# A linear-attention and expert-attention kernel: the last batch's output rows in another buffer, and the last store's second half on another queue

## The chip, the core and the metric

The kernel runs on one core of a Trainium2 chip. The metric is the device time of one execution, in microseconds (us), lower is better. The engines are named as in the profile: PE is TensorE's matmul part and PEld its weight loads, DVE is VectorE, ACT is ScalarE, POOL is GpSimd and SP is SyncE, which here does nothing but issue transfers (DMAs) and wait. An engine's name with a q behind it (SPq, ACTq) means its sequencer, the part that takes instructions in program order, waits for semaphores and issues DMAs.

## What is computed

Two blocks follow each other, for 8 batches of 576 tokens. The first is linear attention without a softmax, normed per head. The second gives its output, as a 576 x 512 matrix, to four attention experts of which each token uses two. Cut to what matters:

```python
kv = np.einsum('bhsd,bhse->bhde', k, v)
out = np.einsum('bhsd,bhde->bhse', q, kv)
x = out / np.sqrt(np.mean(out * out, -1, keepdims=True) + 1e-06) * g_norm
# x as (8, 576, 512); logits = x @ w_gate; the two largest of four, softmax w
for e in range(4):
    a = softmax(causal(scale * (x @ wq[e]) @ (x @ wk[e]).T))
    result += w[e] * (a @ (x @ wv[e]) @ wo[e])     # only where e was chosen
```

The result is 8 x 576 x 512 float32, 9.44 MB, and it is written to HBM block by block.

## The kernel before, in words

A batch's 576 tokens are cut into five blocks: four of 128 and one of 64 (`blocks`, L141). Each step of the work is a small function that emits a few instructions for one batch and one block or head pair. The order in which steps are emitted is written out by hand in the string `ORDER` (L27), the engine that does a copy in `ENGINE` (L53), and the number of the buffer that each new tile gets in `SLOTS` (L67). Each engine runs its own instructions in the order of emission. A step that takes a buffer waits until what had been in it is read.

The buffers of interest:

- `buf(key, ...)` (L174): the first use of a key takes the next digit of `SLOTS`, and the tile lies in the SBUF buffer named after the key's first word and that digit. A tile for `("y", b, qc)` is one output block, 128 x 512 float32, and there are four such buffers, y0 to y3. Those for `("k", b)` hold a whole batch of k, 8 KB in each of 128 partitions, and there are two, k0 and k1.
- PSUM has eight banks, which `small` (L169) hands out by the same string. `own_waits` (L812) makes a step wait for other engines' earlier use of its bank.

The end of each batch is what the change touches. For each head pair, `pv` (L699) multiplies the attention weights with v, `rc`, `iv` and `oc2` (L721, L725, L731) scale the result into the tile `osc`, `ot` (L745) transposes it on TensorE, and `ot_copy` (L753) moves the transposed piece into `OT`. For the last batch, `ot` and `ot_copy` are split in two parts, of the blocks 0 to 2 and 3 to 4. Then, for each of the five blocks, `y_mm` (L758) multiplies by the output weights into a PSUM bank, `y_copy` (L769) copies the bank into a y buffer (on ACT or DVE, as `ENGINE` says), and `store` (L773) issues the transfer to HBM on SP. The block of 64 tokens is computed as two halves of 256 columns, which lie one above the other on 128 partitions, so its store is two transfers of 64 KB each.

The steps at the end of the last two batches (6 and 7) are emitted in the order below; the engine of a copy stands in brackets, and the y buffer that it takes behind it. "y 7,1" is `y_mm` of batch 7 and block 1, "yc" its copy and "st" its store.

```
yc 6,4 [DVE] y2   yc 6,3 [DVE] y1   yc 6,2 [ACT] y3   yc 6,1 [ACT] y0
y 6,0  ...  yc 6,0 [ACT] y2    st 6,0
y 7,1    y 7,2    yc 7,1 [ACT] y1
ot 7,1,1    y 7,0    otc 7,1,1 [ACT]    st 7,1    yc 7,2 [DVE] y3
y 7,4    st 7,2    yc 7,0 [ACT] y0    y 7,3    st 7,0
yc 7,3 [ACT] y2    st 7,3    yc 7,4 [DVE] y1    st 7,4 (two transfers)
```

So the copy of block 7,4 takes the buffer y1 that block 7,1 had. Some PSUM banks matter too: y 6,0 and y 7,2 use the same bank, so y 7,2 starts when yc 6,0 has read it.

The k buffers at that time: k1 held batch 6's k, which the matmuls of `kv` (L397, profile line L405) read; the last matmuls of that line start at 152.4 us.

Of the kernel before, what the change touches and what calls it, by code (L numbers as in the profile page):

```python
# [10 lines left out]
FP32 = mybir.dt.float32  # L11
# [5 lines left out]
NB, NCH, EP, NF = 5, 4, 2, 4  # L17
# [51 lines left out]
    "03213023001450125330041553671046715124206076504703012002312304131301521310305463730144000161154030511021123100"  # L69
    "21032031300212304020355310033454230511002671100030021301312130131233012011162710120630302105741002011007622113"  # L70
    "76237645370022034133033513001020167021101712013140501230131220522000011345101132110062711036712067201230130130"
    "0130210201126701672451030121067001267145340621"
)


# [43 lines left out]
def kernel(  # L119
# [13 lines left out]
    nc = tc.nc  # L133
    P = nc.NUM_PARTITIONS
    B, H, S, Dh = q.shape
    D = H * Dh
# [14 lines left out]
    tiles = {}  # L151
# [6 lines left out]
    def place(key):  # L158
        if key not in slot_of:
            slot_of[key] = int(SLOTS[begun[0]])  # L160
            begun[0] += 1
        return slot_of[key]
# [6 lines left out]
    def small(*key):  # L169
        n = place(("sm",) + key)  # L170
        touched.add(n)
        return pairs[n // 2][:, n % 2, :]

    def buf(key, shape, dtype, name):  # L174
        if key not in tiles:
            n = place(key)
            tiles[key] = sb.tile(shape, dtype, tag=f"{key[0]}{n}", name=f"{name}{n}")
        return tiles[key]
# [102 lines left out]
    def copy(task, dst, src):  # L281
        if engine[task] == "A":
            nc.scalar.copy(dst, src)  # L283
        else:
            nc.vector.tensor_copy(out=dst, in_=src)  # L285
# [472 lines left out]
    def y_mm(b, qc):  # L758
        p_y, (s0, nq) = small("y", b, qc), blocks[qc]
        for pr in range(EP):  # L760
            lhs = OTs[b % 2][:, pr * S + s0 : pr * S + s0 + nq]
            for o in range(P // nq):
# [3 lines left out]
                    start=(pr == 0), stop=(pr == EP - 1), skip_group_check=True,  # L766
                )

    def y_copy(b, qc):  # L769
        w = D * blocks[qc][1] // P  # L770
        copy(("yc", b, qc), buf(("y", b, qc), [P, D], FP32, "y")[:, 0:w], small("y", b, qc)[:, 0:w])

    def store(b, qc):  # L773
        s0, nq = blocks[qc]
        for o in range(P // nq):
            w = D * nq // P
            nc.sync.dma_start(out[b, s0 : s0 + nq, o * w : (o + 1) * w], tiles["y", b, qc][o * nq : (o + 1) * nq, 0:w])

    emit = dict(
        lk=lk, lv=lv, lkr=lkr, lvr=lvr, lq=lq, gr=gr, g8=g8, gb=gb, wg=wg, lw=lw, ws=ws, lwo=lwo, wo=wo,  # L780
# [1 line left out]
        out=out_mm, oc=o_copy, sq=square, red=red, ln=ln, rs=rs, na=newton_a, nb=newton_b, nc=newton_c, nd=newton_d, gl=gl, lg=lg, xm=xm, x=x_tr, xc=x_copy,  # L782
        m8=m8, sh=sh, ex=ex, md=md, mk=mk, gt=gt, den=den, rd=rd, gate=gate, v=v_mm, vc=v_copy,
        qp=lambda b, pr: proj("q", b, pr), kp=lambda b, pr: proj("k", b, pr), qpc=q_proj_copy, kpc=k_proj_copy,
        sc=sc, exp=exp, msk=msk, pv=pv, rc=rc, iv=ivm, oc2=o_scale, ot=ot, otc=ot_copy, y=y_mm, yc=y_copy, st=store,
    )

# [78 lines left out]
```

## Time and profile before

| what | value |
|---|---|
| median of four runs | 226.44 us (225.45 to 227.54) |
| the profiled execution's own time | 225.64 us |
| its span, first to last instruction | 223.9 us |
| PE busy | 208.6 us (93% of the span) |
| DVE busy | 157.6 us (70%) |
| ACT busy | 133.2 us (59%) |
| POOL busy | 126.0 us (56%) |
| stores of results | 48 transfers, all issued by SP |
| HBM written | 9.44 MB |

The profiled execution is 0.80 us below the median. What lies outside its span (225.64 - 223.9) is 1.74 us. The timeline gives each instruction, or run of like instructions, with its start and duration in us from the span's start; "[2.00 <-DMA ...]" behind it is the time for which its engine sat idle before it, and what ended that. A DMA row of SPq or ACTq is the issue alone; the time from the start of the issue to the landing of the data is a view of its own.

### The profile page before, as it was taken

To read this page: it belongs to the slowest core of one execution; us is meant where nothing else is said; L and a number is where in the kernel's file an instruction comes from. 1 tells how busy PE (TensorE), PEld (TensorE's weight loads), DVE (VectorE), ACT (ScalarE), POOL (GpSimd) and SP (SyncE) were. 2 spreads that over 40 slices of the span, in tenths; PEclk is the share of its full clock that TensorE was granted. 3 is DMA by queue.
4 is the path that set the end of the run, shared out by engine and by line. 5 is a ranking of instruction groups with operands and counts; after the bars stand their busy time and mean duration, and the time that the engine had idled before them with its cause. 6 is when DMAs were issued, how large, how long until landed. Compare 5 with 4: busy or idle time off the path is not lost. (4 is left out here: it accounts for less than half of the span.)

```text
span 223.9 us, 6608 instructions
## 1 busy us (share of the span) xinstructions
PE 208.6 (93%) x2550; PEld 177.5 (79%) x2562; DVE 157.6 (70%) x366; ACT 133.2 (59%) x265; POOL 126.0 (56%) x278
## 2 busy tenths in 40 slices
PE   7788799998999989999999999999999999999981
PEld 2467697987998889898997899788878999799550
DVE  6275669749665988789797675499996476843570
ACT  0214742876679462868426954956764982664951
POOL 8400776069538681669607960577649779621620
PEclk9999999999999999999999999999999999999998
DMA  4979979999999879999999899997234000140065
GB/s 124 316 231 259 296 190 221 353 241 128 142 336 241 152 177 273 187 187 218 220 249 241 268 224 234 146 225 157 62 104 147 3 0 4 46 165 3 0 220 207
DMA packets 92577, 40.29 MB, mean 180 GB/s; under 512 B 66689, under 2 KB 88193, under 8 KB 92545
## 3 DMA queue, kind: packets, MB, share of 16 engines
q1 hardware_dynamic: 90784, 38.68, 71.3%
q10 hardware_dynamic: 1632, 1.18, 2.0%
q8 instruction: 20, 0.33, 0.7%
q14 instruction: 13, 0.10, 0.2%
q0 software_dynamic: 128, 0.01, 0.0%
HBM read 30.42 MB, written 9.44 MB: 178 GB/s over the span
## 5 line engine op out<-in xcount | busy, mean ns | idle before, releaser
L686 ACT ACTIVATE PT<-p 128x1024 bf16<-128x1024 f32 (+1 forms) x64 | 50.3, 841 | 6.6 <-PE p L672 6.1
L692 POOL TENSOR_SCALAR_AFFINE_SELECT PT<-PT 128x256 bf16<-128x256 bf16 (+1 forms) x80 | 29.3, 384 | 26.2 <-ACT PT L686 24.9
L557 POOL TENSOR_TENSOR x_tok<-o_sb,rstd 128x512 fp32r<-128x512 f32 x40 | 43.1, 1131 | 0.5
L466 PE MATMUL p<-kvx,qT 128*128 128x136 f32 (+1 forms) x320 | 39.3, 285 | 1.1 <-DVE kvx L285 0.7
L466 PEld LDWEIGHTS p<-kvx,qT 128*128 128x128 f32 (+1 forms) x320 | 34.7, 179 | 3.9 <-DVE kvx L285 0.9
L502 DVE TENSOR_REDUCE ms<-sq 128x8 f32<-128x520 f32 (+1 forms) x40 | 27.0, 684 | 7.5 <-POOL sq L498 3.7
L498 POOL TENSOR_TENSOR sq<-o_sb 128x512 f32<-128x512 f32 (+1 forms) x20 | 20.6, 1041 | 12.6 <-DVE ms L502 6.4
L626 PE MATMUL p<-wv_r,xT 128*128 128x256 f32 x160 | 25.2, 292 | 0.7 <-ACT xT L283 0.7
L567 PE MATMUL p<-ident_r,x_tok 128*128 128x128 f32 (+1 forms) x160 | 23.4, 279 | 0.7 <-DVE vext L285 0.3
L567 PEld LDWEIGHTS p<-ident_r,x_tok 128*128 128x128 f32 x160 | 20.6, 191 | 3.7 <-POOL x_tok L557 1.0
L672 PE MATMUL p<-qTp,kT 64*128 64x64 f32 (+4 forms) x192 | 21.8, 341 | 1.2 <-DVE kT L285 0.5
L283 ACT COPY o_sb<-p 128x544 f32<-128x544 f32 (+1 forms) x29 | 15.1, 532 | 13.0 <-PE p L466 12.5
L626 PEld LDWEIGHTS p<-wv_r,xT 128*128 128x128 f32 x160 | 20.9, 189 | 1.9 <-ACT xT L283 0.8
L645 PE MATMUL p<-xT,wk_r 128*128 128x288 f32 x128 | 20.8, 305 | 0.0
L405 PE MATMUL p<-v_b,k_b 128*64 128x64 f32 x512 | 20.1, 224 | 0.1
L764 PE MATMUL p<-wo_b,OT 128*128 128x512 bf16 (+1 forms) x85 | 18.3, 343 | 1.8 <-issue 0.5
L645 PE MATMUL p<-xT,wq_r 128*128 128x288 f32 x128 | 19.8, 300 | 0.0
L405 PEld LDWEIGHTS p<-v_b,k_b 128*64 128x64 f32 x512 | 17.8, 138 | 2.5 <-issue 2.1
L672 PEld LDWEIGHTS p<-qTp,kT 64*128 64x128 f32 x192 | 14.1, 185 | 6.3 <-ACT PT L686 1.5
L645 PEld LDWEIGHTS p<-xT,wk_r 128*128 128x128 f32 x128 | 17.6, 188 | 1.5 <-DVE xT L285 0.5
L285 DVE COPY o_sb<-p 128x544 f32<-128x544 f32 (+1 forms) x19 | 12.0, 630 | 9.5 <-PE p L466 4.2
L645 PEld LDWEIGHTS p<-xT,wq_r 128*128 128x128 f32 x128 | 17.5, 188 | 0.4 <-issue 0.4
(111 smaller groups left out, 345.5 us busy)
## 6 DMA issues: line engine op xcount, KB each, us to landing
out_dram<-y SPq DMA_DIRECT2D x32, 256.0 KB, 2.7
k_b<-in_k_dram SPq DMA_DIRECT2D x14, 512.0 KB, 5.9
v_b<-in_v_dram SPq DMA_DIRECT2D x14, 512.0 KB, 5.8
q_b<-in_q_dram SPq DMA_DIRECT2D x48, 144.0 KB, 4.7
q_b<-in_q_dram SPq DMA_DIRECT2D x16, 128.0 KB, 3.8
k_b<-in_k_dram SPq DMA_DIRECT2D x4, 256.0 KB, 5.5
v_b<-in_v_dram ACTq DMA_DIRECT2D x4, 256.0 KB, 5.4
k_rem<-in_k_dram SPq DMA_DIRECT2D x16, 64.0 KB, 4.5
```

Source lines behind the costliest of these rows:

```text
L405: nc.tensor.matmul(p_kv[hh * Dh : (hh + 1) * Dh, c, :], lhsT=lhs, rhs=rhs, start=(j == 0), stop=(j == NF), skip_group_check=True,)
L466: nc.tensor.matmul(p_o[p0 : p0 + nt, c // 2, c % 2 * 256 : c % 2 * 256 + 2 * GW], lhsT=qTs[b % NQT][:, c * S + i * P : c * S + i * P + nt] ...
L498: nc.gpsimd.tensor_tensor(out=dst, in0=src, in1=src, op=AluOpType.mult)
L502: nc.vector.tensor_reduce(mss[b % 2][:nt, i, :], sqs[(NB * b + i) % 3][:nt], axis=AX_X, op=AluOpType.add)
L557: nc.gpsimd.tensor_tensor(out=buf(("x", b, i), [P, NCH, P], FP32R, "x_tok")[:].rearrange("p c (h r) -> p h r c", h=H), in0=ob[:, i, :, 0:D ...
L567: nc.tensor.matmul(p_t[:, c * P : c * P + nt], lhsT=tiles["x", b, i][:, c, :], rhs=ident_r[:, 0:nt], start=True, stop=True)
L626: nc.tensor.matmul(p_v[:, 0 : E * Hd], lhsT=blocks_of(xTs[b % 2], c)[:, i * P : (i + 1) * P], rhs=w_r["v"][:, c, :, :].rearrange("p e f -> ...
L645: nc.tensor.matmul(p_p[:, s, 0:HALF], lhsT=w_r[nm][:, c, 2 * pr : 2 * pr + 2, :].rearrange("p e f -> p (e f)"), rhs=blocks_of(xTs[b % 2], ...
L672: nc.tensor.matmul(p_s[:, el, o : o + hi - lo], lhsT=kTs[(2 * b + pr) % 3][pp, kb * P : (kb + 1) * P], rhs=tiles["qTp", b, pr][pp, lo:hi], ...
L686: nc.scalar.activation(PT[:, :, d0 : d0 + o], big("sc", b, pr, j)[:, :, 0:o], ACTF.Exp, scale=scale)
L692: nc.gpsimd.affine_select(out=d, in_=d, compare_op=AluOpType.is_ge, fill=0.0, base=0, pattern=[[0, 2], [1, w]], channel_multiplier=-1,)
L764: nc.tensor.matmul(p_y[o * nq : (o + 1) * nq, 0:w], lhsT=lhs, rhs=wo_b[:, pr, o * w : (o + 1) * w], start=(pr == 0), stop=(pr == EP - 1), ...
```

## The change

Blocks 0 to 3 of the last batch no longer take four y buffers. They share one tile in buffer k1, [128, 4, 512] float32, a slice for each block, and block 4 of the last batch is then the only one of its batch in a y buffer. With three fewer buffer requests, the end of `SLOTS` is shorter: the last digits now give k1 to the shared tile, and still give y1 to block 7,4. The order of the steps and the engines of the copies are as they were. The second of the two transfers of the last block's store (`o` = 1, columns 256 to 511, partitions 64 to 127) is issued by ACT in place of SP; it stands behind yc 7,3 in ACT's order.

```diff
-    "0130210201126701672451030121067001267145340621"
+    "0130210201126701672451030121067001267145461"
 )
...
+    def y_t(b, qc):
+        if b == B - 1 and qc < NF:
+            return buf(("k", "y"), [P, NF, D], FP32, "k_b")[:, qc]
+        return buf(("y", b, qc), [P, D], FP32, "y")[:]
+
     def y_copy(b, qc):
         w = D * blocks[qc][1] // P
-        copy(("yc", b, qc), buf(("y", b, qc), [P, D], FP32, "y")[:, 0:w], small("y", b, qc)[:, 0:w])
+        copy(("yc", b, qc), y_t(b, qc)[:, 0:w], small("y", b, qc)[:, 0:w])
 
     def store(b, qc):
         s0, nq = blocks[qc]
         for o in range(P // nq):
             w = D * nq // P
-            nc.sync.dma_start(out[b, s0 : s0 + nq, o * w : (o + 1) * w], tiles["y", b, qc][o * nq : (o + 1) * nq, 0:w])
+            eng = nc.scalar if b == B - 1 and o else nc.sync
+            eng.dma_start(out[b, s0 : s0 + nq, o * w : (o + 1) * w], y_t(b, qc)[o * nq : (o + 1) * nq, 0:w])
```

## The prediction, made before the change was run

> **What bounds the kernel now.** The page comes first, to see whether the change can reach the bulk of the time:
>
> ```profile
> span 223.9 us, 6608 instructions
> PE 208.6 (93%) x2550; PEld 177.5 (79%) x2562; DVE 157.6 (70%) x366; ACT 133.2 (59%) x265; POOL 126.0 (56%) x278
> PE   7788799998999989999999999999999999999981
> DMA  4979979999999879999999899997234000140065
> ```
>
> PE is 93% busy and full in nearly every slice up to the last two. The change moves nothing that PE does and nothing ahead of the last batch's output, so those 216 us stay. What it can touch is the last slice and a half, where PE falls to 8 and 1: a drain of matmuls, copies and stores. Next, therefore, the chain that ended last, in order of time, from 216 us:
>
> ```profile
> 216.01 0.70 PE p L764 x2
> 216.78 0.59 ACT y L283
> 217.39 2.06 DMA out_dram<-y
> 219.63 0.42 DVE y L285
> ```
>
> This reads: block 7,1's matmuls, its copy on ACT, its store to HBM, and then the copy of block 7,4, which needs the y buffer that this store had to read. It looks as if that wait set the end. Whether it does is decided by SP, so I read the timeline of the same stretch, engine by engine (ACT, DVE, PE), and then SP's three last issues, each in a window of its own:
>
> ```profile
> 216.12 1.24 ACT L283 COPY y<-p 128x512 f32<-128x512 f32 x2 [2.00 <-DMA out_dram<-y]
> 218.00 0.32 ACT L283 COPY OT<-p 128x192 bf16<-128x192 bf16 x1 [0.64 <-PE p L764]
> 218.22 0.59 ACT L283 COPY y<-p 128x512 f32<-128x512 f32 x1
> 219.40 0.59 ACT L283 COPY y<-p 128x512 f32<-128x512 f32 x1 [0.59 <-PE p L764]
> ...
> 217.46 0.69 DVE L285 COPY y<-p 128x512 f32<-128x512 f32 x1 [0.88 <-PE p L764]
> 219.63 0.42 DVE L285 COPY y<-p 128x256 f32<-128x256 f32 x1 [1.49 <-DMA out_dram<-y]
> ```
>
> ```profile
> 218.37 0.41 PE L764 MATMUL p<-wo_b,OT 128*64 128x256 bf16 x4 [0.46 <-ACT OT L283]
> ...
> 218.71 0.60 PE L764 MATMUL p<-wo_b,OT 128*128 128x512 bf16 x2
> ```
>
> ```profile
> 220.01 0.33 SPq L777 DMA_DIRECT2D out_dram<-y  x1
> ...
> 220.43 0.47 SPq L777 DMA_DIRECT2D out_dram<-y  x1
> ...
> 220.96 0.59 SPq L777 DMA_DIRECT2D out_dram<-y  x1
> ```
>
> The reader is to see two things. First, two copies waited for a store's landing: yc 6,0 (216.12) and yc 7,4 (219.63). Second, SP takes its stores in order, and st 7,3 stands ahead of st 7,4. It cannot be issued before yc 7,3 ends on ACT (219.40 + 0.59 = 219.99); it goes at 220.01 and takes 0.33, and the two halves of st 7,4 follow at 220.43 and 220.96. yc 7,4 had ended at 219.63 + 0.42 = 220.05, so it lay finished for 0.38 us before SP got to it. The end is set by yc 7,3 and three issues in a row. The views of time to landing for these three windows give 2.0, 1.9 and 2.0 us: the last data land at 220.96 + 2.0 = 223.0, and 0.9 us of closing instructions bring the span to 223.9.
>
> **The buffer part, step by step.**
> - yc 7,1 (ACT, 216.78): it follows yc 6,0, which ends at 216.12 + 0.59 = 216.71, and its matmuls end at 216.01 + 0.70 = 216.71 too. A free buffer can give at most the 0.07 us in between; I take 0. Its new wait is for the last reader of k1: matmuls of line L405, which start no later than 152.4 us, 64 us earlier. Behind it on ACT stand the OT copy and yc 7,0, so a late one would be felt; it isn't late.
> - yc 7,2 (DVE, 217.46): its idle time is ended by PE. 0.
> - yc 7,0 (ACT, 218.22): it starts while the OT copy (218.00 + 0.32) still ends, back to back. 0.
> - yc 7,3 (ACT, 219.40): ended by PE, whose matmuls finish at 218.71 + 0.60 = 219.31. 0.
> - yc 7,4 (DVE): its matmuls end at 218.37 + 0.41 = 218.78. DVE's previous copy started about 0.08 us after PE was done (217.46 against 216.76 + 0.60 = 217.36), so it starts near 218.87 in place of 219.63 and ends near 219.29, 0.76 us earlier. Nothing waits for it but st 7,4, which SP can't issue before 220.43. So on the path this is 0: the in-order store of 7,3 is the cover, and what is late next.
> - yc 6,0 keeps its buffer y2, whose store (st 6,4) it waited for. That stall stays, and it matters: y 7,2 takes the PSUM bank that yc 6,0 reads. The waits after 215.9 us have it:
>
> ```profile
> ACT y L283 <- DMA out_dram<-y: 2.0, 1, 2.0
> DVE y L285 <- DMA out_dram<-y: 1.5, 1, 1.5
> PEld L764 <- ACT y L283: 0.4, 1, 0.4
> ```
>
> The change removes the second of these waits, which is covered, and leaves the first and third, through which PE's last matmuls, yc 7,3 and the end are late.
>
> **The queue part.** SP loses one issue of 0.59 us. Half a, its last, still starts at 220.43 and lands 1.9 later, near 222.35. The end moves by the distance of the two starts, 220.96 - 220.43 = 0.53, and up to 0.1 of the difference in landing (2.0 against 1.9, both rounded): 0.53 to 0.63. I take 0.55, near the part that is not rounding.
>
> That holds if half b, now on ACT, lands before half a. The trace has no store issued by ACT, so I bound it.
> - Start: yc 7,4 is done near 219.29, and ACT's program reaches the issue after yc 7,3. If the sequencer goes on while that copy runs, the issue starts near 219.45; if it has to wait for its end, near 220.02.
> - Landing: the seven stores issued from 216.7 us on landed in 1.9 to 2.1 us. ACT's own last issues, four loads in the opening, landed in 4.5 to 5.8, beside loads on the other queues. So b lands between 219.45 + 1.9 = 221.35 and 220.02 + 5.8 = 225.8. I take 2.0, because the tail has no other traffic than these stores, as those seven had: 221.5 to 222.0. Then a decides. The far end costs 225.8 - 223.0 = 2.8.
> - Collision: issues on the two queues at once may slow each other. In the opening, ACT's issues of v took 0.48 to 0.62 with SP issuing beside them, and 0.37 for one whose start fell into a pause of SP. So up to 0.25 on SP's issue of 7,3 or of a. If b starts at 219.45 and takes 0.59 as on SP, it ends at 220.04, as SP starts: 0. I take 0 and keep 0.25.
> - ACT has no work behind this issue, so nothing is held up by it.
>
> A rule of the Trainium skill speaks against this part. "DMA: Bandwidth & Descriptors", section "Rules for kernel authors", says of two transfers to disjoint partition halves not to bother, since they serialize on the same 16 DMA engines; read strictly, the end stays at 223.0 and the gain is 0. In this trace the halves' landings are as far apart as their issues, which looks like the issuing rather than the data. The same page, "Issuing engines are not separate DMA queues", grants the second queue just the issue time, which would give 0.59.
>
> **The sum.** Buffer 0 (0 to 0.07), queue 0.55 (0.63 to a loss of 2.8). The profile would go from a span of 223.9 to 223.35, and its time from 225.64 to 225.1. The runs' median lies 0.80 above the profiled execution, so the median forecast is 226.44 - 0.55 = 225.9.
>
> **The rivals.**
> 1. No gain, 226.4. Half b lands as late as before: a landing of 3.55 us or more from 219.45 does it. For it: the views of single stores between 212.39 and 213.70 show 3.6, 3.5 and 3.5 us, with stores in quick succession. Against: the stores of the last 7 us, all near 2.0.
> 2. Slower, ACT's queue as slow as in its opening rows: 226.44 + 2.8 = 229.2. For it: nothing was issued there since 5.2 us. Against: those loads shared 16 engines that the page shows busy. It decides once b lands after 223.0.
> 3. Slower, because four blocks share a tile. If a copy had to wait for the landing of the store of another slice, yc 7,2 would wait for st 7,1 (219.44) and start at 219.63, its store go at 220.34 and land at 222.4; yc 7,0 then ends at 223.2, lands 225.25; yc 7,3 ends at 226.0; half a, 0.42 after st 7,3's issue, starts at 226.5 and lands at 228.4, against 223.0: +5.4, 231.9. It decides if yc 7,2 starts over 2 us late. Against it: slices of a tile pass independently now. DVE writes one part of osc from 214.44 while PE transposes another from 214.58, with no wait for each other (timelines of both).
> 4. More than forecast: if the wait of yc 7,4 (1.49) were on the path as the chain draws it, its 0.76 would come off besides: 226.44 - 0.55 - 0.76 = 225.1. Against it: SP's order above.
>
> **How the numbers follow.** The forecast has 0.74, rival 1 0.12, rival 2 0.04, rival 3 0.04, rival 4 0.06. The predicted time is 225.9. The four runs before lie from 0.99 below to 1.10 above their median, and a new median can be off by as much: 225.9 - 1.1 = 224.8 is the low end, which holds rival 4 too. Upward, rival 1 (226.4) plus 0.25 for colliding issues, plus some 0.4 of scatter, gives 227.1; rivals 2 and 3 (0.08) stay outside. One per cent is 2.3 us, about what a measurement of this kernel can tell from no change. The forecast and rivals 1 and 4 lie within it, rivals 2 and 3 above it. From scatter I add 0.08 to faster, where forecast and rival 4 lean, and take one of rivals 2 and 3's 0.08 off, as b may land less late than the far row: faster 0.08, same 0.85, slower 0.07.
>
> **What would show it.** In the profile after: yc 7,4 starts near 218.9 and waits for PE, not a DMA; SP's last issue is half a, near 220.4, 0.4 after st 7,3; ACT issues half b between 219.4 and 220.1, and it lands before half a; yc 6,0 still waits for a store; the span is near 223.35. I am wrong if ACT's issue or its landing takes over 3 us, if any of yc 7,1 to 7,3 waits for a DMA, or if something earlier than 216 us moves.

## The result, and the profile after

| | before | after |
|---|---|---|
| median, all runs | 226.94 us (55 runs, 224.83 to 231.15) | 226.22 us (36 runs, 224.44 to 228.62) |
| ratio to the kernel before | | 0.9983, 95% interval 0.9964 to 1.0003 |
| profiled execution | 225.64 us, span 223.9 | 227.40 us, span 225.7 |

The ratio means 0.17% or 0.4 us off, with an interval from 0.8 us off to 0.1 us on: too little to be told from no change by the time alone. Executions more than 1.5% above the fastest one of their kernel are left out of the ratios.

The profiled execution of the changed kernel is longer than that of the kernel before, although its end is shorter. The page's head:

```profile
span 225.7 us, 6603 instructions
PE 210.0 (93%) x2550; PEld 177.9 (79%) x2562; DVE 157.0 (70%) x366; ACT 133.4 (59%) x265; POOL 126.1 (56%) x278
PE   7797799999999999999989999999999999999991
PEclk9699999999999999999999999999999999999999
```

The second digit of PEclk, 6, is new. Busy time by stretches of 2 us, first before, then after (columns: stretch, length, busy time of PE, PEld, DVE, ACT and POOL with instruction counts, granted clock, DMA share, GB/s):

```profile
8.00:10.00 2.00, 2.00 (x16) 0.81 (x14) 0.00 (x0) 0.00 (x0) 0.16 (x1) 1.00 1.10 340
10.00:12.00 2.00, 2.00 (x41) 1.69 (x43) 0.67 (x3) 0.00 (x0) 0.00 (x0) 1.00 1.10 348
```

```profile
8.00:10.00 2.00, 2.00 (x6) 0.63 (x5) 0.00 (x0) 0.00 (x0) 0.16 (x1) 0.50 1.12 303
10.00:12.00 2.00, 2.00 (x10) 0.51 (x6) 0.00 (x0) 0.00 (x0) 0.00 (x0) 0.71 1.10 348
```

In this execution the granted clock was 0.50 and 0.71 where it had been 1.00, and PE did 6 and 10 matmuls in place of 16 and 41. From 15 us on, ACT's instructions run 2.2 us later than before, from 48 us on 1.9 us, and from 117 us to the tail 2.5 us later; the last step, of 0.6 us, falls where the clock is full, and its cause is not shown. None of it comes from the change, which emits nothing there that is not emitted before: the profiles of e2 and e4 below, kernels that begin with the same instructions, have a granted clock of 1.00 from 6 to 14 us, and in e2 the tail begins at 211.6 us (before: 211.9, after: 214.4). So the two spans must not be compared; the tails can. For the tail I use two lengths: from SP's first issue of st 6,4 (the store whose second half yc 6,0 waits for) to the start of yc 7,3 on ACT, and from there to the last landing.

ACT, DVE and SP in the tail of the changed kernel (timelines; SP's last two issues each in a window of its own):

```profile
218.13 0.59 ACT L283 COPY y<-p 128x512 f32<-128x512 f32 x1 [1.48 <-DMA out_dram<-y]
219.30 0.59 ACT L283 COPY k_b<-p 128x512 f32<-128x512 f32 x1 [0.58 <-PE p L764]
...
221.65 0.59 ACT L283 COPY k_b<-p 128x512 f32<-128x512 f32 x1 [0.55 <-PE p L764]
221.65 0.55 ACTq L784 DMA_DIRECT2D out_dram<-y  x1
```

```profile
219.76 0.69 DVE L285 COPY k_b<-p 128x512 f32<-128x512 f32 x1 [0.65 <-PE p L764]
221.17 0.42 DVE L285 COPY y<-p 128x256 f32<-128x256 f32 x1 [0.72 <-ACT k_b L283]
```

```profile
222.26 0.33 SPq L784 DMA_DIRECT2D out_dram<-k_b  x1
...
222.68 0.47 SPq L784 DMA_DIRECT2D out_dram<-y  x1
```

Block 7,4's copy (221.17) starts 0.48 us ahead of yc 7,3 (221.65); before, it started 0.23 us behind it. The view puts the end of its idle time down to ACT, whose copy of block 7,0 ends at 221.10; its own matmuls end at 221.07. Which of the two it waited for can't be told, but it is no longer a DMA. No copy into k1 waits for a DMA. ACT issues half b in the same moment in which its copy starts, so its sequencer does not wait for the engine. SP's last issue is half a, 0.42 after st 7,3. Half b lands at 223.74, half a at 224.78. From the start of yc 7,3 to the last landing it is 3.13 us; before it was 223.00 - 219.40 = 3.60.

The chain that ended last, from 220.6 us (start, us, what), now ends with yc 7,3 and not with a store and yc 7,4:

```profile
220.66 0.96 PE p L764 x6
221.62 0.02 issue
221.65 0.59 ACT k_b L283
```

### The profile page after: what moved, and what is told of

Same layout as the page of the kernel before. It is cut to its first block, busy times and chain, and to the rows that moved or that the text cites. A ratio compares the mean times of both kernels' runs of the same rounds, so it can differ in the third digit from the quotient of the medians.

```text
span 225.7 us, 6603 instructions
## 1 busy us (share of the span) xinstructions
PE 210.0 (93%) x2550; PEld 177.9 (79%) x2562; DVE 157.0 (70%) x366; ACT 133.4 (59%) x265; POOL 126.1 (56%) x278
```

## The experiments

Two lengths of each kernel's tail, in us from its trace, and the ratio of its time to the kernel before. "Landing" is that of st 6,4's second half, from the first issue of st 6,4. e5b and e6b are the kernels of e5 and e6 in a second profile.

| kernel | landing | first issue of st 6,4 to yc 7,3 | yc 7,3 to last landing | ratio (95%) |
|---|---|---|---|---|
| before | 4.15 | 7.53 | 3.60 | |
| after | 3.64 | 7.25 | 3.13 | 0.9983 (0.9964 to 1.0003) |
| e1_queue_only | 4.22 | 7.60 | 3.17 | 0.9971 (0.9931 to 1.0012) |
| e2_buffer_only | 3.86 | 7.25 | 3.60 | 0.9982 (0.9946 to 1.0017) |
| e3_one_transfer | 3.85 | 7.29 | 5.87 | 1.0105 (1.0069 to 1.0141) |
| e4_swap | 3.87 | 7.25 | 2.94 | 0.9967 (0.9927 to 1.0006) |
| e5_swap_queue | 3.55 | 7.29 | 3.79 | 1.0023 (0.9984 to 1.0062) |
| e5b_swap_queue | 3.65 | 7.29 | 3.79 | one run |
| e6_k0 | 4.14 | 7.25 | 3.29 | 0.9995 (0.9958 to 1.0032) |
| e6b_k0 | 3.55 | 7.25 | 3.25 | one run |
| e7_k0_swap | 4.05 | 7.25 | 2.94 | 0.9981 (0.9941 to 1.0021) |
| e8_both_act | 3.96 | 7.30 | 3.08 | 0.9987 (0.9945 to 1.0029) |
| e10_third_issue | 3.62 | 7.29 | 3.75 | one run |

The ratios are uncertain by 0.2 to 0.4%, 0.4 to 0.9 us; only e3 is clear of 1. What is said below rests on the tails. In the two kernels that were profiled twice they repeat to 0.04 us (3.79 and 3.79, 3.29 and 3.25); the landing does not (4.14 and 3.55 in e6).

**The queue part alone.** Kernel before, with this edit:

```diff
-            nc.sync.dma_start(out[b, s0 : s0 + nq, o * w : (o + 1) * w], ...)
+            eng = nc.scalar if b == B - 1 and o else nc.sync
+            eng.dma_start(out[b, s0 : s0 + nq, o * w : (o + 1) * w], ...)
```

> Only the queue part: the y buffers are those of the kernel before, and the second half of the very last store is issued by ACT. Measured from the start of yc 7,3 on ACT to the landing of the last store (before: 219.40 to 223.0, 3.6 us; after: 221.65 to 224.8, 3.1 us). My theory, that SP's in-order issues set the end: 3.1 us, as in the changed kernel, and a ratio near 0.998 to the kernel before; yc 7,4 still waits for the landing of st 7,1 and starts some 0.2 us after yc 7,3, and the half on ACT is issued near 0.7 us after that start and lands near 2.7, before SP's half. Rival, that the buffer is what counts: 3.6 us and a ratio of 1.000.

The last landing came at 3.17 us. The timelines of DVE, ACT and SP:

```profile
221.42 0.42 DVE L285 COPY y<-p 128x256 f32<-128x256 f32 x1 [1.48 <-DMA out_dram<-y]
```

```profile
221.20 0.59 ACT L283 COPY y<-p 128x512 f32<-128x512 f32 x1 [0.59 <-PE p L764]
221.88 0.56 ACTq L778 DMA_DIRECT2D out_dram<-y  x1
```

```profile
222.23 0.47 SPq L778 DMA_DIRECT2D out_dram<-y  x1
```

The wait for the buffer is there as before (1.48 us), ACT issues half b later (221.88), and the end is shorter all the same: SP's half a is the last, 1.03 after the start of yc 7,3. So the queue alone gives nearly all of the shorter tail, 0.43 of 0.47 us.

**The buffer part alone.** Changed kernel, with all stores on SP:

```diff
-            eng = nc.scalar if b == B - 1 and o else nc.sync
+            eng = nc.sync
```

> Only the buffer part: blocks 0 to 3 of the last batch go to k1, all stores are on SP. My theory: from the start of yc 7,3 to the last landing 3.6 us, as before, ratio 1.000, although yc 7,4 no longer waits for a store and starts some 0.5 us ahead of yc 7,3. Rival, that the wait in the chain was on the path: 3.1 us or less and a ratio of 0.998 or below.

3.60 us, to a hundredth that of the kernel before:

```profile
218.36 0.42 DVE L285 COPY y<-p 128x256 f32<-128x256 f32 x1 [0.71 <-ACT k_b L283]
218.84 0.59 ACT L283 COPY k_b<-p 128x512 f32<-128x512 f32 x1 [0.55 <-PE p L764]
```

```profile
219.87 0.47 SPq L784 DMA_DIRECT2D out_dram<-y  x1
...
220.40 0.59 SPq L784 DMA_DIRECT2D out_dram<-y  x1
```

yc 7,4 ends at 218.78 and its store is issued 1.1 us later, behind st 7,3. The wait that the chain of the kernel before ended with was no part of what set the end.

**One transfer in place of two.** Kernel before, with:

```diff
+        if (b, qc) == (B - 1, NF):
+            w = D * nq // P
+            nc.sync.dma_start(out[b, s0 : s0 + nq, :].rearrange("s (o w) -> o s w", w=w), tiles["y", b, qc][:, 0:w])
+            return
```

> The kernel before, with the two halves of the very last store as one transfer from 128 partitions on SP. My theory, that the number of issues on SP sets the end: this one is issued 1.0 us after the start of yc 7,3, its issue takes 0.33 to 0.6 us, and it lands at 3.0 to 3.2 us, as in the changed kernel, without ACT; ratio near 0.998. Rival, that the work of issuing goes with the rows and not with the transfers: an issue of 1.06 us (0.47 + 0.59), a landing near 3.6 us, and a ratio of 1.000.

Both theories missed. The issue took 0.63 us, close to what mine allowed, but the kernel is slower by 1.0%, clear of noise:

```profile
219.56 0.63 SPq L777 DMA_DIRECT2D out_dram<-y  x1
```

The trace has no landing for this store; SP's wait for it ended 4.83 us after its issue, and the 5.87 us of the table go to that end. Two stretches in which this store, and in the kernel before the last three stores, are the only large transfers (columns as above):

```profile
221.30:224.30 3.00, 0.00 (x0) 0.00 (x0) 0.00 (x0) 0.00 (x0) 0.00 (x0) 0.50 0.12 38
```

```profile
221.30:222.80 1.50, 0.00 (x0) 0.00 (x0) 0.00 (x0) 0.00 (x0) 0.00 (x0) 1.00 0.53 146
```

A DMA share of 0.12 is that of two of 16 DMA engines busy all the time, and in the trace two packets are in flight at a time for most of that stretch. That fits a rule of the Trainium skill ("DMA: Bandwidth & Descriptors", section "Why a DMA increments its semaphore by 16 and not by 1"): the number of engines goes by the slowest dimension of each access pattern, which in HBM is the two halves here. So one issue fewer was no gain where the transfer then ran on two engines.

**The cover taken away: st 7,4 ahead of st 7,3.** Changed kernel, and:

```diff
     order, engine = unpack(B)
+    order.remove(("st", B - 1, NF - 1))
+    order.append(("st", B - 1, NF - 1))
```

> The changed kernel, with st 7,4 ahead of st 7,3 in SP's order, so that the cover of the earlier yc 7,4 is gone. My theory: SP issues its half of 7,4 about 0.05 us before yc 7,3 starts, st 7,3 0.6 us after that start, and the last landing is at 2.6 to 2.7 us (3.1 in the changed kernel); ratio to the kernel before near 0.996. Rival, that landings of several stores close together stretch (3.5 us near 213 us in the kernel before): 3.1 us or more, no better than the changed kernel.

2.94 us, between the two theories. The stretch's timeline:

```profile
219.86 0.47 SPq L786 DMA_DIRECT2D out_dram<-y  x1
219.88 0.59 ACT L285 COPY k_b<-p 128x512 f32<-128x512 f32 x1 [0.55 <-PE p L766]
219.89 0.56 ACTq L786 DMA_DIRECT2D out_dram<-y  x1
220.49 0.47 SPq L786 DMA_DIRECT2D out_dram<-k_b  x1
```

The starts are as expected, but the half on ACT landed 2.34 us after its issue and st 7,3 2.33 (2.01 before); st 7,3's issue took 0.47 in place of 0.33. The two halves, issued within 0.03 us of each other, landed 0.42 us apart. So stores in flight together took longer from issue to landing, by some 0.3 us here.

**The same order without the other buffer.**

> The queue part with st 7,4 ahead of st 7,3 on SP, but with the y buffers of the kernel before, so that yc 7,4 still waits for the landing of st 7,1. Beside e4_swap it tells what the other buffer is worth once its cover is gone. My theory: yc 7,4 ends 0.65 us after the start of yc 7,3, SP's half goes at 0.67 and st 7,3 near 1.2, and the last landing is at 3.2 to 3.5 us (e4_swap: 2.9), so the buffer is worth 0.3 to 0.6 in this order; ratio near 0.998. Rival, that the buffer is worth nothing in any order: 2.9, as e4_swap.

That profile has a mean granted clock of 0.97; a second one of the same kernel:

> e5_swap_queue once more, since the profile of its first run was taken at a mean granted clock of 0.97 and a span of 229.9 us. My theory: the same tail, the last landing 3.8 us after the start of yc 7,3, since nothing in it is bound by TensorE. Rival, that the lower clock made the tail longer: 3.2 to 3.5 us, as first expected.

Both profiles give 3.79 us, at 0.97 and 0.99 of the clock, so the clock was not the reason that my 3.2 to 3.5 was too low.

```profile
221.47 0.58 ACT L285 COPY y<-p 128x512 f32<-128x512 f32 x1 [0.59 <-PE p L766]
221.90 0.42 DVE L287 COPY y<-p 128x256 f32<-128x256 f32 x1 [1.68 <-DMA out_dram<-y]
222.35 1.10 SPq L780 DMA_DIRECT2D out_dram<-y  x2
222.35 0.56 ACTq L780 DMA_DIRECT2D out_dram<-y  x1
```

yc 7,4 starts 0.43 after yc 7,3, not 0.23 as in the one profile that I had worked from, in which yc 7,3 itself was late (7.53 against 7.29 us); and st 7,3 waits behind half a. Against e4_swap the other buffer is worth 3.79 - 2.94 = 0.85 us in this order, and nothing behind yc 7,3 in the order of the change (e2).

**The remaining wait of yc 6,0 removed.** Changed kernel, and block 0 of batch 6 in k0 (its digit in `SLOTS` goes from 2 to 0):

```diff
+        if (b, qc) == (B - 2, 0):
+            return buf(("k", "y6"), [P, NF, D], FP32, "k_b")[:, 0]
```

> The changed kernel, and block 0 of batch 6 goes to a buffer of its own in k0, so that yc 6,0 no longer waits for the landing of st 6,4's second half. In five profiles the time from SP's first issue of st 6,4 to the start of yc 7,3 was 7.53 (before), 7.25 (after), 7.60, 7.25 and 7.29 us, the longer ones where that half landed latest. My theory: 7.25 or a little less whatever the landing, the last landing 3.1 us after the start of yc 7,3; a ratio of 0.996 to 0.998. Rival, that the spread has another cause: it stays between 7.25 and 7.6 with no link to a wait, ratio as in the changed kernel.

The second profile of this kernel:

> e6_k0 once more, since the profile of its first run was taken at a mean granted clock of 0.989. My theory: 7.25 us from the first issue of st 6,4 to the start of yc 7,3, and 3.1 to 3.3 us from there to the last landing. Rival: another time than 7.25 in an undisturbed execution.

```profile
216.86 0.59 ACT L283 COPY k_b<-p 128x512 f32<-128x512 f32 x1 [1.20 <-PE p L764]
```

yc 6,0 now waits for PE, and 7.25 us holds in three profiles of this buffer, with landings of 3.55, 4.14 (the first profile) and 4.05 us (e7). Where yc 6,0 still waits, 7.25 to 7.30 holds up to a landing of 3.96, and then every later landing comes through: 4.15 gives 7.53 and 4.22 gives 7.60. The last landing was 3.25 us, 0.1 over the changed kernel's; why is not shown. The ratio shows no gain.

> e6_k0 with the order of e4_swap: both remaining waits of the tail are gone. From the first issue of st 6,4 to the start of yc 7,3 at most 7.25 us, from there to the last landing 2.9 us; the sum, 10.15 us, is 1.0 below the kernel before (7.53 + 3.60 = 11.13), ratio near 0.995.

7.25 and 2.94, a sum of 10.19 against 11.13: the tail shrank by 0.94 us, near the 1.0 expected; 0.24 of it is the late landing in the one profile before. The time did not show it: 0.9981, with an interval that holds 0.995 and 1.

**Both halves on ACT.**

```diff
-            eng = nc.scalar if b == B - 1 and o else nc.sync
+            eng = nc.scalar if (b, qc) == (B - 1, NF) else nc.sync
```

> The changed kernel, with both halves of the very last store issued by ACT; the order is as in the changed kernel. My theory: ACT issues the halves at 0.0 and 0.5 us after the start of yc 7,3, SP only st 7,3 at 0.6 us, and the last landing is at 2.7 to 2.95 us (3.1 in the changed kernel), the upper end if landings stretch as in e4_swap (2.3 in place of 2.0); ratio near 0.996. Rival, that ACT's second issue waits for the copy on its own engine to end: issue at 0.6 to 1.2 us, last landing 3.2 us or later.

```profile
221.43 0.59 ACT L283 COPY k_b<-p 128x512 f32<-128x512 f32 x1 [0.55 <-PE p L764]
221.44 0.56 ACTq L784 DMA_DIRECT2D out_dram<-y  x1
...
222.04 0.62 ACTq L784 DMA_DIRECT2D out_dram<-y  x1
```

3.08 us lies between the two theories' times and is hardly better than the change's 3.13. ACT's issues start at 0.01 and 0.60 us. The first does not wait for the copy on its engine. The second follows the end of the first by 0.04 and the end of the copy by 0.02, so the trace does not tell which of them it waited for. Its half lands 2.48 us after its issue, beside two other stores.

**One issue more.** Kernel before, half b as two transfers of 32 rows:

```diff
+            for h in range(2 if (b, qc, o) == (B - 1, NF, 1) else 1):
+                n = nq // 2 if (b, qc, o) == (B - 1, NF, 1) else nq
+                r = h * n
+                nc.sync.dma_start(
+                    out[b, s0 + r : s0 + r + n, o * w : (o + 1) * w],
+                    tiles["y", b, qc][o * nq + r : o * nq + r + n, 0:w],
+                )
```

> The kernel before, with the second half of the very last store cut in two of 32 rows each, so that SP issues three transfers behind st 7,3: the suspected cost once more, with the same data. My theory, that the issues in a row on SP set the end: the last issue starts 0.4 to 0.65 us later than in the kernel before, near 2.1 us after the start of yc 7,3, and the last landing is near 4.1 us (before: 3.6). Rival, that the data or its landing sets it: the smaller last piece lands at 3.6 us or before.

```profile
219.06 0.59 ACT L283 COPY y<-p 128x512 f32<-128x512 f32 x1 [0.59 <-PE p L764]
```

```profile
221.25 0.41 SPq L780 DMA_DIRECT2D out_dram<-y  x1
```

The third issue starts 2.19 us after yc 7,3, 0.63 later than the last one before, as mine had it. It lands at 3.75, 0.15 later, as neither had it: a piece of half the size landed 1.56 us after its issue in place of 2.04. So "issues in a row" is right for the starts, and the landing is no constant. The issues grew by 0.63 us and the end by 0.15.

## Why the prediction came out as it did, point by point

- **The size.** The forecast was 0.55 us off, 225.9 from a median of 226.44. The time moved by 0.4 us with an interval from 0.8 off to 0.1 on, which can't tell 0.55 from 0. The absolute time, 226.22, lies in the range; but the median before, over 55 runs, is itself 0.5 us above the four runs that I started from, so that nearness shows little. The same mechanism, from that base, would have been 226.94 - 0.55 = 226.4. The span of the one profile, 225.7 and not near 223.35, says nothing either way: what lies ahead of 216 us did move, a sign of being wrong that the prediction had named, but in this execution and not by the change.
- **"I take 0.55"**, the queue part: this is the term that was mis-sized. In the traces it is 0.47 (3.60 to 3.13), and 0.43 with the queue part alone (3.17). The distance of the issues was as worked out: SP's last starts 1.03 us after yc 7,3 in place of 1.56, 0.53 earlier. What failed is the landing of half a, taken at 1.9 us as in the kernel before, with **"Collision ... I take 0"**. The issues were not slowed (0.33 and 0.47), but half a landed 2.10 us after its issue in place of 1.95, and st 7,3 2.12 in place of 2.01. So the landing, which was to add up to 0.1 to the 0.53, took 0.06 off it (2.10 against half b's 2.04 before). It goes with half b on ACT's queue: half a took 2.10 to 2.26 us in the four profiles that have it there ahead of half a (the changed kernel, e1, e6, e6b), and 1.93 to 1.95 in the three that have it behind half a on SP (before, e2, e10). In e4 two other stores show the effect at 0.3.
- **"Buffer 0 (0 to 0.07)"**: shown by e2 for the end (3.60 both). Upstream it gives 0.04: where the landing is not late, the length up to yc 7,3 is 7.25 with the other buffer and 7.29 without. It lies in yc 7,3, taken at 0: the copy starts 0.04 us after its matmuls end in all seven profiles with the other buffer and 0.08 in all six without. The reason that it hides, SP's order, is shown by e4 against e5b.
- **Half b on ACT**: issued at the early end of the bounds, at the start of yc 7,3, and landed in 2.08 us. That it lands ahead of half a (1.04 us) held, so what rivals 1 and 2 rest on, a late half b, did not happen.
- **"That stall stays, and it matters"**, of yc 6,0: half right. It stays (1.48 us idle), but it reaches yc 7,3 only in profiles where st 6,4's second half lands over 3.9 us after the first issue. In the profile before it cost 7.53 - 7.29 = 0.24; in that after, nothing. I took one execution's stall for a fixed one.
- **Rival 3**, a whole tile tracked as one: fell, the copies into k1 wait for PE alone. **Rival 4**, the chain's wait on the path: fell by e2.
- **The skill's rule that two halves serialize** is half borne out: issued together they land 0.42 us apart (e4; 0.33 in e5b), issued in a row on one queue 0.62 (2.98 and 3.60), so the distance is not the issuing alone. Read strictly, with a gain of 0, it did not hold for the tail, which ends 0.47 us earlier. Its advice, one transfer, cost 1.0% here (e3), on two DMA engines.

What stays open: whether the change gains anything in the time. Two tails 0.5 us apart are shown; that the time follows is not, nor is it for e7, whose tail is 0.9 us shorter. The ratio of the change, 0.9983, is no sign of it: e2, with the tail of the kernel before (3.60), has 0.9982. The scatter of single executions, 224.4 to 228.6 us for the changed kernel, is several times the difference of the tails, and most of it arises ahead of them: in these thirteen profiles SP's first issue of st 6,4 comes anywhere from 211.2 (e3) to 217.9 us (e5). In the changed kernel's the clock from 8 to 12 us explains most of its delay; in the others the granted clock from 6 to 14 us is 1.00.

## What to carry to other kernels

A wait that the chain of the profile ends with is only on the path if nothing in front of its consumer is later: here the finished block stood in SP's queue behind a store whose data were not ready. At the end of a kernel, count the issues in a row on the last queue and what each waits for, and change buffers and order together: here neither shortened the end alone (the buffer 3.60 in e2; the order, with half b on ACT, 3.79 in e5 against 3.17 in e1), and both did (2.94 in e4). And compare tails from a common event, not spans, when what a change can give is smaller than the scatter of all that comes ahead of them.

## What was not expected of the hardware

- The granted clock fell to 0.50 between 8 and 10 us in one execution and in none of the other twelve profiles, and what followed ran some 2 us later, four times what the change does.
- The time from the end of an issue to the landing went with the size of a store: 1.68 us for 256 KB (2.01 - 0.33), 1.45 for 64 KB (2.04 - 0.59), 1.15 for 32 KB (1.56 - 0.41), in the kernel before and e10.
- Issuing 64 rows of 1 KB took longer, 0.47 and 0.59 us, than issuing 128 rows of 2 KB, 0.33; right behind half a those 128 rows took 0.47 to 0.54 as well (e4, e5, e5b, e7).
